# Linear attention and a gated MLP on one core: k and q projected apart in all pairs, transfers planned to land later, another order

## The chip, the cores and the metric

The kernel runs on one core of a Trainium2 chip. The metric is the device time of one execution in microseconds. TensorE (PE, with its weight loads as PEld), VectorE (DVE), ScalarE (ACT), GpSimd (POOL) and SyncE (SP, which issues nearly all DMAs) each run their own instructions in the order in which the program lists them, and wait for each other by semaphores.

## What is computed

The reference, cut to what matters:

```python
def _attn_ref(q, k, v, omega):          # q, k, v: (8, 8, 576, 64), omega: (128, 64)
    scale = 1.0 / np.sqrt(np.sqrt(D))
    def phi(x):
        proj = np.einsum('bhsd,md->bhsm', x, omega)
        h = proj - np.sum(x * x, axis=-1, keepdims=True) / 2.0
        h = h - np.max(h, axis=-1, keepdims=True)
        return np.exp(h) / np.sqrt(m)
    q_p, k_p = phi(q * scale), phi(k * scale)
    kv = np.einsum('bhsm,bhsd->bhmd', k_p, v)
    z = np.sum(k_p, axis=2)
    num = np.einsum('bhsm,bhmd->bhsd', q_p, kv)
    den = np.einsum('bhsm,bhm->bhs', q_p, z)[..., None] + 1e-06
    return num / den
def _moe_ref(x, w_in, w_out):           # x: (4608, 512), w_in: (512, 2048), w_out: (2048, 512)
    h = x @ w_in
    return (h / (1.0 + np.exp(-h))) @ w_out
```

The result of the attention, with its heads side by side, is the `x` of the MLP.

## The kernel before

**The attention** is worked off in 32 pairs of heads (`n` = 0 to 31, four pairs to a batch). For each pair, `project` (L393) multiplies the raw k or q by omega in 8 matmuls of 128 columns. Each contracts over 64 rows, and two heads share the array as a tile of rows 0 to 63 and one of rows 64 to 127; the trace shows each of these fp32 matmuls as two instructions, so 16 for k and 16 for q. The results fill two PSUM banks for k and two for q. A further small piece, `project_mids` (L419), projects the block that both heads share, on the full array. DVE takes maxima (`top`) and makes the biases (`shift`), ACT takes the exponentials out of PSUM (`expo`, L462) and so sets the banks free. Then come the sum over k (`sums` on POOL, `zsum` on PE, L513), k times v (`kv`, L521, in column tiles of 64), a transposition of it (`kv_turn`, L529), the denominators (`denom` on DVE, L545), the normalisation (`normal`, L556), three transpositions of q's features (`turn`, L562) and the numerator (`numer`, L583, in column tiles). The next pair's `kv` and a pair's `numer` stand together as one unit, `kvnum`.

**The MLP** is the bulk of the matmuls, all at L754 (`thrice`): 3120 instructions on the full array with 512 columns. Stages 1 and 2 work tile by tile of 512 tokens; later tiles are taken in pairs, by a seven-product scheme whose inner parts are the units `deep` and `product` (6 matmuls each). Attention pieces are pushed in between L754's all along, until about 813 us.

**What sets the order.** Every step is a unit with an engine, a guessed duration, a due time (`key`), the units that it comes after, and the buffers that it takes and frees. `Plan.run` (L170 to L318) plays these units through with its own guesses and emits them in that order; each engine then runs its share in that order. Four things in it matter here:

- `STIR` (L80): a table of (seed, size, from, to, mask). At L173 it moves the due times of some units by a pseudo-random amount. It only changes the order.
- `BOTH` (L38): for pairs in it (18 to 31) the k and the q projection are one unit that needs four free banks at once (L933 to L938); for the others they are two units of two banks each (L939 to L943).
- Banks: attention pieces take PSUM banks from `att` (2 banks) and, late in the program, from `h` (2 banks; L209). A unit is placed when the plan has its banks free.
- Transfers: a unit with `lat` on SP is taken to have landed at `max(pipe, t + dur + 2.2)` (L296 to L298), where `pipe` serialises the transfers and a large load has `lat` 1.5. What uses the data is planned from then on.

`TURN` (L113, 0.2) is the plan's price for a change of PE between full array, row tiles and column tiles; it stays.

Of the kernel before, what the change touches and what calls it, by code (L numbers as in the profile page):

```python
# [34 lines left out]

LAG = 2
FOLD = tuple(range(8))
BOTH = tuple(range(18, 32))  # L38
DIRECT = {(n, who) for n in range(28) for who in "kq" if not 8 <= n < 12}
NORM_DVE = tuple(range(8, 12))  # L40
AHEAD_OUT = 3
# [36 lines left out]
HANDOFF = {"PE": 0.3, "ACT": 0.25, "DVE": 0.22, "POOL": 0.2, "SP": 0.2}  # L78
CALM = 0.5
STIR = (  # L80
# [30 lines left out]
)  # L111
BOND = 0.0
TURN = 0.2  # L113
WIDE = ("w", "ts", "xq", "c", "ic", "g0", "g1", "g2", "g3")
TINY = ("mxk", "mxq", "nbk", "nbq", "mxm", "nbm", "sq", "den", "rd")
LEADIN = 96
# [36 lines left out]
class Plan:  # L153
# [16 lines left out]
    def run(self):  # L170
# [9 lines left out]
        pipe = port = 0.0  # L180
# [50 lines left out]
        while any(ready.values()):  # L231
            best = None
            for e, us in ready.items():
                pick, least = None, None
                for u in us:
                    t = 0.0
                    for a in u["after"]:
                        if self.units[a]["eng"] == e and not self.units[a]["lat"]:
                            t = max(t, end[a])
                        else:  # L240
                            t = max(t, first[a] + (CALM if e == "PE" and t > START_MLP else 0.0))
                    ok = True
                    for ring, _ in u["alloc"]:
# [4 lines left out]
                        t = max(t, s)  # L248
                    pools = ()
                    if ok and u["banks"]:  # L250
                        pools, s = bank_pools(u)
                        ok = pools is not None
                        if ok:
                            t = max(t, s)
                    if not ok:
                        continue
                    t = max(t, free_at[e])
                    if u["port"] and e == "POOL":
                        t = max(t, port)
                    elif u["port"]:  # L260
                        for a, b in holds:
                            if a <= t < b:
                                t = b
# [13 lines left out]
            u, pools, _, t = best  # L277
            e, n = u["eng"], u["name"]
            ready[e].remove(u)
            dur = u["dur"]  # L280
# [3 lines left out]
            if e == "PE":  # L284
                if tiled_by(u) != mode:
                    dur += TURN
                mode = tiled_by(u)
# [7 lines left out]
            done = t + dur  # L295
            if u["lat"]:  # L296
                pipe = max(pipe, t + dur + 1.0) + u["lat"]
                done = max(pipe, t + dur + 2.2)  # L298
            end[n] = done
            first[n] = done + HANDOFF[e]  # L300
            for ring, i in u["alloc"]:
# [20 lines left out]
def attention_mlp(ctx: ExitStack, tc: tile.TileContext, qT, kT, qn, kn, v, om_in, w_in, w_out, out):  # L322
# [581 lines left out]
    for n in range(NWIN):  # L904
# [3 lines left out]
        for i, who in enumerate("kq"):  # L908
# [23 lines left out]
            pj_after = [("raw",) + w, "omega"] + ([("r2",) + w] if fold else [])  # L932
            if n in BOTH:  # L933
                if i == 0:
                    add(pj, "PE", 1.75, at(n, 0, o + 3), lambda a, b, c, d, n=n: (project(n, "k", a, b), project(n, "q", c, d)),
                        banks=4, after=[("raw", n, x) for x in "kq"], order=[("proj", n - 1, x) for x in ("k" if n - 1 in BOTH else "kq")],
                        alloc=[("hk", ("h", n, "k"))] + [(f"{t}{x}", (t, n, x)) for t in ("mx", "nb") for x in "kq"])
            else:  # L938
                add(pj, "PE", 1.9 if fold else 1.15 if n < 2 * NPAIR else 0.9, at(n, 3 * i, o),  # L939
                    lambda a, b, n=n, who=who: project(n, who, a, b), banks=2, after=pj_after,  # L940
                    order=([("proj", n - 1, "k" if n - 1 in BOTH else who)] if n else []) + ([("mids", n)] if i and not fold else []),
                    alloc=([(f"h{who}", ("h",) + w)] if fold or not i else []) + ([] if fold else [(f"mx{who}", ("mx",) + w)])
# [4 lines left out]
            for j in range(3 if fold else 2):  # L947
                add(("top", n, who, j), "DVE", 0.2 if j == 2 else 0.6,
                    at(n, 3 * i + 1 + 0.1 * j, o + 1.2 + 0.1 * j),
                    lambda n=n, who=who, j=j: top(n, who, j), after=[md if j == 2 else ("proj", n, "k") if n in BOTH else pj])  # L950
            if not fold:
# [4 lines left out]
        if not fold:  # L956
# [8 lines left out]
            plan.freed_by[("raw", n, "k")] = [("mids", n), ("proj", n, "k")]  # L965
            plan.freed_by[("raw", n, "q")] = [("mids", n), ("proj", n, "k" if n in BOTH else "q")]
        e = {}
# [484 lines left out]
```

## Time and profile before

| | before |
|---|---|
| median of 3 runs | 989.75 us (985.5 to 991.65) |
| profiled execution, its own time | 988.49 us |
| its span, first to last instruction | 986.7 us |
| PE busy | 957.2 us (97%) |
| DVE, ACT, POOL busy | 771.4 us, 642.7 us, 403.5 us |
| granted TensorE clock | 1.000 |

In the rows that follow, a matmul's start is measured and its end is modelled, so the time of a stretch of PE is best read from one start to a later one. A row of the timeline has start, length, engine, line, operation, tiles, shape and count, and in brackets the idle time before it with what ended it. `ps_att`, `ps_h` and `ps_acc` are PSUM banks by pool, `rawk` and `rawq` the raw k and q, `oms` the scaled omega.

### The profile page before, as it was taken

Reading aid. Unit: us, or ns where it says so; the run is one execution under the profiler, and the core shown is the slowest. Engines: PE = TensorE matmul, PEld = TensorE weight load, DVE = VectorE, ACT = ScalarE, POOL = GpSimd, SP = SyncE. Lnnn points to the kernel's source line nnn. Section 1 sums busy time; section 2 is a strip of 40 time slices with the busy share of each in tenths; the row PEclk is TensorE's granted clock in tenths of the full one; section 3 lists DMA queues with packets and bytes.
Section 4 is the critical chain, followed back from the end, with each engine's and each line's share of the span. In section 5 each row is a group of like instructions: output and inputs, shape, how many; then the busy total and the mean of one; then the engine's idle time right before and its main releaser. Section 6 shows DMA issues by size and latency. Waiting matters only on the chain.

```text
span 986.7 us, 17025 instructions
## 1 busy us (share of the span) xinstructions
PE 957.2 (97%) x5846; PEld 767.6 (78%) x5846; DVE 771.4 (78%) x1611; ACT 642.7 (65%) x1237; POOL 403.5 (41%) x427
## 2 busy tenths in 40 slices
PE   8899899999999999999999999999999999999998
PEld 7677677777777777787788888788888878888886
DVE  3998798689455889884888999788799976369954
ACT  7998886688787776668568866566284544325442
POOL 3765465677876657776341343213111220000000
PEclk9999999999999999999999999999999999999999
DMA  7588887799998788898667666576555566556662
GB/s 283 196 270 284 287 293 255 258 376 316 303 291 288 265 284 270 324 305 289 218 211 236 196 206 225 203 268 201 170 181 192 192 201 229 192 192 214 194 214 103
DMA packets 103735, 238.70 MB, mean 242 GB/s; under 512 B 13665, under 2 KB 44513, under 8 KB 103649
## 3 DMA queue, kind: packets, MB, share of 16 engines
q1 hardware_dynamic: 103504, 237.54, 71.6%
q8 instruction: 47, 0.77, 0.3%
q14 instruction: 40, 0.32, 0.1%
q10 hardware_dynamic: 144, 0.07, 0.0%
HBM read 193.53 MB, written 44.04 MB: 241 GB/s over the span
## 4 chain that ended last, share of the span: by engine, by line
PE 64%; DVE 17%; ACT 8%; DMA 6%; issue 3%; POOL 1%; SPq 0%; DVEq 0%; ACTq 0%; POOLq 0%
PE ps_acc L754 47%; PE ps_h L754 5%; DVE prod L545 3%; DVE g L792 2%; PE ps_h L401 2%; PE ps_att L401 2%; ACT hq L462 2%; DVE g L654 2%; PE ps_att L521 2%; DVE g L650 1%; DVE ts L800 1%; DMA ic<-w_d 1%; DVE g L648 1%; ACT hk L462 1%; DMA g<-w_out 1%
## 5 line engine op out<-in xcount | busy, mean ns | idle before, releaser
L754 PE MATMUL ps_acc<-ts,w 128*128 128x512 f32 x2544 | 614.6, 395 | 0.3 <-issue 0.3
L754 PEld LDWEIGHTS ps_acc<-ts,w 128*128 128x128 f32 x2544 | 468.5, 188 | 97.5 <-issue 0.7
L796 ACT CAST ts<-g 128x1024 fp32r<-128x1024 f32 x112 | 118.6, 1063 | 101.2 <-PE ps_acc L754 95.0
L800 DVE TENSOR_TENSOR ts<-g,ts 128x1024 fp32r<-128x1024 f32 x112 | 144.4, 1294 | 48.6 <-ACT ts L796 48.2
L754 PE MATMUL ps_h<-xq,w 128*128 128x512 f32 x576 | 149.6, 401 | 3.5 <-ACT g L787 1.9
L556 POOL TENSOR_TENSOR hq<-hq,rd 128x384 f32<-128x384 f32 x84 | 89.7, 1094 | 110.8 <-DVE rd L551 109.6
L754 PEld LDWEIGHTS ps_h<-xq,w 128*128 128x128 f32 x576 | 104.1, 189 | 26.1 <-ACT g L787 3.1
L846 DVE TENSOR_TENSOR g<-ps_acc,g 128x512 f32<-128x512 f32 x144 | 95.2, 685 | 23.8 <-PE ps_acc L754 22.3
L491 POOL TENSOR_TENSOR t<-hk 128x256 f32<-128x256 f32 x64 | 57.6, 916 | 84.7 <-ACT hk L462 42.5
L792 DVE TENSOR_TENSOR g<-g,g 128x1024 f32<-128x1024 f32 x64 | 84.6, 1343 | 6.0 <-ACT g L787 5.7
L545 DVE CUSTOM_DVE_ANT_0 prod<-hq,ps_att 128x128 f32<-128x128 f32 (+1 forms) x180 | 51.6, 287 | 30.4 <-PE ps_att L513 11.4
L504 POOL TENSOR_TENSOR es<-t,es 128x256 fp32r<-128x256 f32 x32 | 28.7, 898 | 91.7 <-ACT es L500 91.7
L850 ACT ACTIVATE g<-g 128x1024 f32<-128x1024 f32 x36 | 37.6, 1058 | 32.7 <-DVE g L846 32.5
L668 POOL TENSOR_TENSOR w<-g,w 128x512 fp32r<-128x512 f32 x32 | 42.9, 1355 | 35.0 <-ACT w L664 14.6
L496 POOL TENSOR_TENSOR t<-t,hk 64x128 f32<-64x128 f32 x64 | 39.2, 613 | 20.7 <-ACT hk L462 17.2
L812 ACT CAST ts<-xq 128x1024 fp32r<-128x1024 f32 x21 | 22.2, 1056 | 33.8 <-PE ps_acc L754 31.5
L382 ACT ACTIVATE nat<-nat 128x576 f32<-128x576 f32 x48 | 32.8, 701 | 16.5 <-DMA nat<-kn 14.0
L816 DVE TENSOR_TENSOR ts<-xq,ts 128x1024 fp32r<-128x1024 f32 x21 | 27.0, 1284 | 19.9 <-ACT ts L812 19.9
L873 DVE TENSOR_TENSOR c<-ps_acc,c 128x512 f32<-128x512 f32 x48 | 30.8, 682 | 7.2 <-PE ps_acc L754 7.2
L462 ACT ACT_TABLE_LOAD x22 | 28.2, 1283 | 12.5 <-DVE nbk L441 8.0
L387 DVE TENSOR_REDUCE sq<-nat 128x9 f32<-128x576 f32 x48 | 34.5, 744 | 1.1 <-ACT nat L382 0.8
L462 ACT ACTIVATE hq<-ps_att,nbq 128x128 f32<-128x128 f32 x115 | 32.7, 386 | 4.0 <-DVE nbq L441 3.2
(210 smaller groups left out, 1535.8 us busy)
## 6 DMA issues: line engine op xcount, KB each, us to landing
w<-w_d SPq DMA_DIRECT2D x168, 512.0 KB, 4.2
w<-ws_d SPq DMA_DIRECT2D x48, 512.0 KB, 3.4
rawk<-kT SPq DMA_DIRECT2D x32, 352.0 KB, 4.1
rawq<-qT SPq DMA_DIRECT2D x32, 352.0 KB, 4.5
v<-v SPq DMA_DIRECT2D x32, 320.0 KB, 4.5
out<-c SPq DMA_DIRECT2D x17, 512.0 KB, 4.2
g<-w_in SPq DMA_DIRECT2D x16, 512.0 KB, 5.0
g<-w_out SPq DMA_DIRECT2D x16, 512.0 KB, 4.5
```

The costliest lines, as they stand in the source:

```text
L401: nc.tensor.matmul(ps[:, cols], raw[r, o : o + P], w[r], start=True, stop=n not in FOLD)
L462: nc.scalar.activation(h[:, c], ps[:, i * M : (i + 1) * M], AF.Exp, bias=bias_of(n, who, c), scale=-1.0 if n in FOLD else 1.0)
L491: nc.gpsimd.tensor_tensor(t[:, i], e[:, 5 * i : 5 * i + 2], e[:, 5 * i + 2 : 5 * i + 4], ALU.add)
L496: nc.gpsimd.tensor_tensor(t[r, i - 3, 0], t[r, i - 3, 0], e[r, MID], ALU.add)
L545: nc.vector.tensor_tensor_reduce(out=prod[r], in0=e[r, c], in1=z[r, j * M : (j + 1) * M], scale=1.0, scalar=GUARD, op0=ALU.mult, op1=ALU.a ...
L556: nc.gpsimd.tensor_tensor(e[:, c], e[:, c], rd[:, c].unsqueeze(2).broadcast_to([P, 3, M]), ALU.mult)
L668: nc.gpsimd.tensor_tensor(lo, T["w", i], hi.bitcast(F32), ALU.subtract)
L754: nc.tensor.matmul(ps, w(a), x[:, b], start=first and n == 0, stop=last and n == 2, **more)
L792: nc.vector.tensor_tensor(out, a, b, ALU.subtract)
L796: nc.scalar.copy(g[:, 0], T["g", p, SOURCE[j], u])
L800: nc.vector.tensor_tensor(g[:, 1], T["g", p, SOURCE[j], u], g[:, 0].bitcast(F32), ALU.subtract)
L846: nc.vector.tensor_tensor(to, T["q", p, chain, i], T["g", p, r, i // 2][:, i % 2], ALU.add)
```

## The change

The plan's three inputs change; no function that computes does. All instructions of the matmuls, copies and sums are the same in number; the order on every engine is another, and four more ACT table loads come in (70 to 74 in the program).

```diff
-BOTH = tuple(range(18, 32))
+BOTH = ()
...
 STIR = (
-    (29444, 2.5, -100, 900, 3), (30620, 4.0, -100, 900, 7), (57745, 2.5, 101, 261, 7), (26472, 5.25, 448, 538, 0),
...
+    (3618, 7.5, 64, 144, 7), (32634, 2.5, 89, 249, 0), (95862, 4.0, 338, 498, 3), (19267, 4.9, 349, 379, 0),
...
 TURN = 0.2
+LANDING = 0.9
...
             if u["lat"]:
                 pipe = max(pipe, t + dur + 1.0) + u["lat"]
-                done = max(pipe, t + dur + 2.2)
+                done = max(pipe, t + dur + 2.2) + LANDING
```

The helpers' lines stand one higher in the changed file (L754 is L753 there).

Three places on PE show what moves. The first is pair 21. Before, from the transposition of pair 20's kv to that of its features:

```order
L529 MATMUL ps_att<-ident,kt 128x128
L754 MATMUL ps_acc<-ts,w 128x512 x18
L401 MATMUL ps_h<-oms,rawk 128x128 x8
L401 MATMUL ps_att<-oms,rawq 128x128 x8
L754 MATMUL ps_acc<-ts,w 128x512 x30
L421 MATMUL ps_h<-oms,rawk 128x128
L421 MATMUL ps_h<-oms,rawq 128x128
L562 MATMUL ps_h<-ident,hq 128x128 x3
L754 MATMUL ps_acc<-ts,w 128x512 x6
L562 MATMUL ps_att<-ident,hq 128x128 x3
```

And in the change, from pair 21's k projection on:

```order
L400 MATMUL ps_att<-oms,rawk 128x128 x8
L420 MATMUL ps_h<-oms,rawk 128x128
L420 MATMUL ps_h<-oms,rawq 128x128
L753 MATMUL ps_acc<-ts,w 128x512 x6
L561 MATMUL ps_h<-ident,hq 128x128 x3
L753 MATMUL ps_acc<-ts,w 128x512 x6
L561 MATMUL ps_h<-ident,hq 128x128 x3
L753 MATMUL ps_acc<-ts,w 128x512 x6
L561 MATMUL ps_h<-ident,hq 128x128 x3
L753 MATMUL ps_acc<-ts,w 128x512 x12
L400 MATMUL ps_h<-oms,rawq 128x128 x8
L753 MATMUL ps_acc<-ts,w 128x512 x12
```

The q half of pair 21 now stands by itself between L754's, 30 of them away from its k half.

The second place is the middle block of pair 20. Before, it stands six L754 behind the transposition L529 of pair 19:

```order
L521 MATMUL ps_h<-hk,v 64x128 x10
L583 MATMUL ps_h<-en,kw 64x512 x2
L583 MATMUL ps_h<-en,kw 64x64 x2
L754 MATMUL ps_acc<-ts,w 128x512 x6
L513 MATMUL ps_h<-es,ones 128x256 x2
L529 MATMUL ps_h<-ident,kt 128x128
L754 MATMUL ps_acc<-ts,w 128x512 x6
L421 MATMUL ps_h<-oms,rawk 128x128
L421 MATMUL ps_h<-oms,rawq 128x128
```

In the change the middle block stands ahead of `kvnum`, and the transposition comes after both:

```order
L753 MATMUL ps_acc<-ts,w 128x512 x6
L420 MATMUL ps_att<-oms,rawk 128x128
L420 MATMUL ps_att<-oms,rawq 128x128
L520 MATMUL ps_h<-hk,v 64x128 x10
L582 MATMUL ps_att<-en,kw 64x512 x2
L582 MATMUL ps_h<-en,kw 64x64 x2
L753 MATMUL ps_acc<-ts,w 128x512 x6
L528 MATMUL ps_h<-ident,kt 128x128
```

The third place is the q projection of pair 16, which before stands six L754 behind its own middle block and next to pair 17's:

```order
L421 MATMUL ps_att<-oms,rawk 128x128
L421 MATMUL ps_att<-oms,rawq 128x128
L754 MATMUL ps_acc<-ts,w 128x512 x6
L401 MATMUL ps_att<-oms,rawq 128x128 x8
L401 MATMUL ps_h<-oms,rawq 128x128 x8
```

In the change the three transpositions of pair 15 and 18 L754's stand between the two, and pair 17's half is not beside it:

```order
L420 MATMUL ps_att<-oms,rawk 128x128
L420 MATMUL ps_att<-oms,rawq 128x128
L561 MATMUL ps_att<-ident,hq 128x128 x3
L753 MATMUL ps_acc<-ts,w 128x512 x6
L561 MATMUL ps_att<-ident,hq 128x128 x3
L753 MATMUL ps_acc<-ts,w 128x512 x6
L561 MATMUL ps_att<-ident,hq 128x128 x3
L753 MATMUL ps_acc<-ts,w 128x512 x6
L400 MATMUL ps_att<-oms,rawq 128x128 x8
L753 MATMUL ps_acc<-ts,w 128x512 x24
```

Counted over PE's whole list past the start-up (that is, from the first L754 on): two projections next to each other 15 times before (pairs 18 to 31, and the q halves of 16 and 17), never in the change; a projection next to a `kvnum` once before, 8 times in the change.

56 rows, old and new, of the table STIR are left out of this document.

## Prediction

> **What bounds the kernel now.** I read the page's busy times first, then the windows by stage, then the waits of PE, then PE's timeline at the places that the change moves.
>
> ```profile
> PE 957.2 (97%) x5846; PEld 767.6 (78%) x5846; DVE 771.4 (78%) x1611; ACT 642.7 (65%) x1237; POOL 403.5 (41%) x427
> PE 64%; DVE 17%; ACT 8%; DMA 6%; issue 3%; POOL 1%; SPq 0%; DVEq 0%; ACTq 0%; POOLq 0%
> ```
>
> PE is busy 97% of the span, and no other engine is over 78%. So there are only two ways to change the time: the matmuls themselves take more or less of PE, or the 29.5 us in which PE is idle (986.7 - 957.2) shrink or grow. The windows, cut at 62 us (start-up over), 325, 475 and 813 us (last attention piece), tell where those 29.5 us lie. The columns after the window's length are busy us with the number of instructions for PE, PEld, DVE, ACT and POOL, then the granted clock, DMA share and GB/s.
>
> ```profile
> 0.00:62.00 62.00, 53.43 (x587) 43.47 (x587) 44.26 (x140) 53.27 (x155) 34.25 (x51) 1.00 0.69 236
> 62.00:325.00 263.00, 250.71 (x1594) 195.50 (x1591) 196.41 (x477) 209.40 (x403) 172.44 (x180) 1.00 0.88 297
> 325.00:475.00 150.00, 145.61 (x936) 115.40 (x935) 122.53 (x267) 106.71 (x238) 104.25 (x97) 1.00 0.84 287
> 475.00:813.00 338.00, 337.77 (x1989) 273.48 (x1989) 295.82 (x606) 207.03 (x371) 92.58 (x100) 1.00 0.62 206
> 813.00:986.70 173.70, 169.63 (x750) 139.72 (x746) 112.34 (x125) 66.28 (x74) 0.00 (x0) 1.00 0.57 191
> ```
>
> PE idles 8.6 us in the start-up, 12.3 us up to 325, 4.4 us up to 475, 0.2 us up to 813, and 4.1 us at the end, most of it behind the last matmul. The change's pairs 18 to 31 lie in the third and fourth window. In the fourth, PE has no idle time to give: whatever is added to PE there is paid in full, and a wait that is taken away there gains nothing.
>
> **What a projection by itself costs.** A lone k half (16 instructions) between L754's, late in the second window:
>
> ```profile
> 324.29 2.20 PE L754 MATMUL ps_h<-xq,w 128*128 128x512 f32 x9
> 326.42 1.16 PE L401 MATMUL ps_att<-oms,rawk 64*128 64x128 f32 x16
> 327.51 2.34 PE L754 MATMUL ps_h<-xq,w 128*128 128x512 f32 x9
> 329.69 0.62 PE L754 MATMUL ps_acc<-ts,w 128*128 128x512 f32 x2
> ...
> 813.38 147.19 PE L754 MATMUL ps_acc<-ts,w 128*128 128x512 f32 x648
> ```
>
> The last row gives the pace of L754 when nothing interrupts it: 147.19 / 648 = 0.227 us. From 324.29 to 329.69 are 5.40 us with 18 of them (4.09 us), so the half costs 1.31 us. Both halves together, pair 21:
>
> ```profile
> 467.38 4.35 PE L754 MATMUL ps_acc<-ts,w 128*128 128x512 f32 x18
> 471.66 1.16 PE L401 MATMUL ps_h<-oms,rawk 64*128 64x128 f32 x16
> 472.66 1.06 PE L401 MATMUL ps_att<-oms,rawq 64*128 64x128 f32 x16
> 473.65 7.10 PE L754 MATMUL ps_acc<-ts,w 128*128 128x512 f32 x30
> 480.59 0.38 PE L421 MATMUL ps_h<-oms,rawk 128*128 128x128 f32 x2
> ...
> 483.01 1.64 PE L754 MATMUL ps_acc<-ts,w 128*128 128x512 f32 x6
> 484.49 0.49 PE L562 MATMUL ps_h<-ident,hq 128*128 128x128 f32 x3
> ```
>
> From 467.38 to 480.59 are 13.21 us with 48 L754's (10.90 us): 2.31 us. The first run stands behind a transposition, which slows it by 0.12 us (483.01 to 484.49: six take 1.48 us, not 1.36), so the two halves cost 2.19 us. Two lone halves cost 2.62 us. Parting them costs 0.43 us, and it is the way into row tiles and back that is paid twice.
>
> The order has 15 such neighbours before (14 pairs, and the q halves of pairs 16 and 17) and none after: 15 x 0.43 = **+6.4 us**. Against it stand projections next to a `kvnum`, once before and 8 times now. There the way out of the one and the way into the other fall together:
>
> ```profile
> 319.74 0.71 PE L583 MATMUL ps_att<-en,kw 128*64 128x512 f32 x6
> 320.38 1.66 PE L754 MATMUL ps_h<-xq,w 128*128 128x512 f32 x6
> 321.88 0.40 PE L513 MATMUL ps_att<-es,ones 128*128 128x256 f32 x2
> ```
>
> Behind a `kvnum` six L754's take 1.50 us (320.38 to 321.88), 0.14 over their pace; ahead of a projection nine take 2.13 us (324.29 to 326.42), 0.09 over. So a direct neighbour saves about 0.2 us: 7 x 0.2 = **-1.4 us**. Net **+5.0 us** of PE, about 3.7 of it for pairs 21 to 31 (11 x 0.43 less 5 x 0.2), past 467 us, where no idle time hides it. Bounds: the part before that, 1.3 us, may lie in waits that exist anyway (+3.7 in all); without the neighbours' saving it is +6.4.
>
> The Trainium skill, page "TensorEngine Tiling (Array Packing)", section "Key Properties", says that changing the tiling mode drains the TensorE, whether between full array and tiles or from one kind of tile to another. By that rule row tiles next to column tiles save nothing and the term would be +6.4; by the rows above, half of the two ways falls away.
>
> **What the waits give back.** PE's waits in the third window, grouped, and then the rows of the timeline at the four longest:
>
> ```profile
> PE ps_h L421 <- ACT kw L534: 1.2, 1, 1.2
> PE ps_h L562 <- POOL ic L711: 1.1, 1, 1.1
> PE ps_att L401 <- ACT hk L462: 0.9, 1, 0.9
> PE ps_att L513 <- ACT kt L526: 0.7, 1, 0.7
> PE ps_att L562 <- ACT en L566: 0.4, 1, 0.4
> ```
>
> ```profile
> 351.43 0.50 PE L513 MATMUL ps_att<-es,ones 128*128 128x256 f32 x2 [0.69 <-ACT kt L526]
> 372.02 1.04 PE L401 MATMUL ps_att<-oms,rawq 64*128 64x128 f32 x13 [0.94 <-ACT hk L462]
> 399.69 0.52 PE L562 MATMUL ps_h<-ident,hq 128*128 128x128 f32 x3 [1.15 <-POOL ic L711]
> 456.26 0.49 PE L421 MATMUL ps_h<-oms,rawk 128*128 128x128 f32 x2 [1.20 <-ACT kw L534]
> ```
>
> The last row is the second place shown in the order: pair 20's middle block waits for the bank of a transposition six L754's ahead, which ACT copies late. In the change the block stands before that transposition: -1.20 us. The second of the four is the third place: a q half that waits for the exponential of its own middle block, six L754's ahead. Now 18 L754's and three transpositions lie between: -0.94 us. At 351.43 the sum over k stands three L754's behind a `kvnum`; in the change it is nine: 6 x 0.227 = 1.36 us more, over the 0.69 that was waited. These three places: **-2.8 us**.
>
> The wait at 399.69 is of another kind. The profile names POOL, but what ends at that time is ACT's work on the bank of pair 18's four-bank projection, which stands ahead of this transposition:
>
> ```profile
> 396.63 0.69 ACT L382 ACTIVATE nat<-nat 128x576 f32<-128x576 f32 x1 [4.65 <-DMA nat<-kn]
> 397.22 1.04 ACT L796 CAST ts<-g 128x1024 fp32r<-128x1024 f32 x1
> 398.16 0.40 ACT L500 CAST es<-t 128x256 fp32r<-128x256 f32 x1
> 398.46 1.91 ACT L462 ACTIVATE hk<-ps_h,nbk 128x128 f32<-128x128 f32 x7
> ```
>
> ```profile
> w<-w_d SPq DMA_DIRECT2D x168, 512.0 KB, 4.2
> ic<-w_d SPq DMA_DIRECT2D x16, 512.0 KB, 5.8
> nat<-kn SPq DMA_DIRECT2D x24, 288.0 KB, 4.0
> ```
>
> ACT stood 4.65 us at a square whose load was late, with the exponentials queued behind it. The plan counts on 2.2 to 2.9 us from issue to use, the rows show medians of 4.0 to 5.8 us; with 0.9 us more it counts on 3.1 to 3.8. And in the change pair 18's projections come behind pair 16's transpositions. I count this wait as gone: **-1.15 us**. All of them: -4.0 of the 4.4 us in that window.
>
> **What may come in.** Each of the 28 half projections now waits for two banks of its own, in order on PE, with all of PE's list queued behind it, and with DVE and ACT behind that. The trace shows no such lone half in the four-bank part. Nearest is the 0.94 us above; none of them wait: 0; all: 26 us. In the fourth window, with the same four banks, PE idles 0.2 us in 338 although four banks had to be free at once, so I take the low end: **+0.5 us**.
>
> In the start-up ACT sets the pace (53.27 of 62 us). Counted over ACT's list up to the copy of pair 3's x, the change has one L636 and two L664 more ahead of it:
>
> ```profile
> L636 ACT ACTIVATE g<-g 128x512 f32<-128x512 f32 x7 | 4.9, 758 | 0.4 <-DMA g<-w_in 0.4
> L664 ACT CAST w<-g 128x512 fp32r<-128x512 f32 x5 | 3.4, 676 | 1.0 <-DVE g L654 0.9
> ```
>
> That is 0.76 + 2 x 0.68 = 2.1 us later for x, and 2.1 us of weight work that no longer stands in the way afterwards. Bounds -2.1 and +2.1; I take 0, since the sum of ACT's work is the same. The four table loads that come in lie past 475 us, where ACT has 131 us to spare; without that cover they would cost about 5 us.
>
> **The sum** goes by the profiled execution: 988.5 + 5.0 - 4.0 + 0.5 = **990.0 us**. That execution is 1.3 us under the median of the three runs shown, 989.75; the three spread over 6 us, so I leave it there. A measurement of this kernel can tell about 1% from no change, that is 9.9 us: below 979.9 is faster, above 999.7 slower.
>
> **The rivals.** (1) The waits up to 325 us go as well. The 12.3 us of idle time there come from the same causes, late loads and banks, and the new order and landing time touch every one of them; a full gain gives 990.0 - 12.3 = 977.7, and it has to take 10 of the 12.3 to count as faster. Against it: the pairs there already had k and q apart, the chain still runs through the same exponentials, and a new order makes waits as well as it removes them. Chance 0.17. (2) The lone halves wait for banks: if 14 of 28 wait 0.94 us each, 990.0 + 13.2 - 0.5 = 1002.7; slower from about 11 of them on. For it: the waits at 372.02 and 399.69 are just this kind. Against it: two banks are found sooner than four. Chance 0.13. (3) The parting costs nothing, because the halves fall into time that PE would wait anyway: 985.0. Against it is the 0.2 us of idle in the fourth window. Chance 0.15. (4) The landing time does nothing, since 3.8 us is still below what the rows show, and the waits move to other pieces: all 4.0 us stay and the time is 994.0. Chance 0.15.
>
> **How the numbers follow.** The forecast itself has 0.40; with (3) and (4), which both end within 1%, 0.70 for no change, 0.17 for faster, 0.13 for slower. The forecast's own range is 985 to 995 by the bounds above. The range to hold 8 of 10 reaches to (1) and most of the way to (2): **978 to 1001 us**, which leaves out rather less than half of each.
>
> **What would show it.** In the profile of the changed kernel: lone L401 rows of 16 in the fourth window, each 1.3 us over L754's pace; PE busy up by about 5 us, to 962; the waits at L421, L401, L513 and L562 of the third window gone, its idle time at 1 us or less; the fourth window's idle time still below 1 us. I am wrong on the price if PE's busy time does not rise; wrong on the waits if idle time between 62 and 475 us differs from about 13 us by more than 5; rival (2) would show as L401 waiting for ACT's L462 many times past 350 us.

## The result and the profile after

| | before | changed |
|---|---|---|
| median | 988.37 us (985.19 to 991.65, 13 runs) | 993.37 us (989.51 to 996.97, 13 runs) |
| ratio to before | | 1.0054, 95% interval 1.0039 to 1.0069 |
| profiled execution, span | 988.49 us, 986.7 us | 994.02 us, 992.1 us |

The change makes the kernel 5.3 us slower by the ratio, which is clear of noise and well inside what was called no change. The forecast of 990.0 us was for a profiled execution of 988.49; the one of the changed kernel took 994.0. Busy times on the page of the changed kernel:

```profile
PE 963.0 (97%) x5846; PEld 772.2 (78%) x5846; DVE 769.0 (78%) x1611; ACT 648.8 (65%) x1241; POOL 404.0 (41%) x427
```

The span is 5.4 us longer. PE's busy time rose by 5.8 us (957.2 to 963.0), its idle time went from 29.5 to 29.1 us. So nearly nothing was won back in waits, and the loss is matmuls that take longer. The windows at the same cuts, with the columns as before:

```profile
0.00:62.00 62.00, 50.49 (x527) 40.94 (x527) 43.22 (x138) 51.37 (x150) 35.83 (x51) 0.97 0.67 231
62.00:325.00 263.00, 253.76 (x1642) 200.30 (x1642) 196.50 (x482) 210.04 (x406) 172.76 (x179) 0.99 0.86 295
325.00:475.00 150.00, 145.99 (x909) 114.57 (x909) 113.99 (x251) 109.05 (x236) 96.11 (x96) 1.00 0.87 287
475.00:813.00 338.00, 338.00 (x2002) 273.10 (x2001) 300.48 (x618) 210.28 (x376) 99.28 (x102) 1.00 0.64 204
813.00:992.10 179.10, 174.75 (x772) 143.30 (x770) 114.79 (x127) 68.08 (x76) 0.00 (x0) 1.00 0.58 194
```

PE idles 11.5 us in the start-up (8.6 before), 9.2 us up to 325 (12.3), 4.0 us up to 475 (4.4), and nothing up to 813 (0.2). The clock column, which stood at 1.00 everywhere before, is below it in the first two windows. Windows at fixed times hold different work in two kernels, so a better measure is when the same L754 starts, counted from the first of the 3120. The number has to be one at which PE has done the same other work in both kernels; the rows below are such numbers (at 12 and 120 one to three small instructions differ). The times in us by which some of them start later than in the kernel before (each from one profiled execution; the two later columns belong to experiments below):

| L754 number, its start before | changed | q six behind k | k and q together again |
|---|---|---|---|
| 12, at 64.0 us | +5.3 | -0.9 | +4.1 |
| 120, at 100.9 us | +7.6 | -0.1 | +6.4 |
| 570, at 264.2 us | -0.2 | 0.0 | -0.9 |
| 754, at 323.8 us | +1.9 | +0.7 | +1.6 |
| 1163, at 459.4 us | +2.8 | +2.5 | +1.4 (at 1170) |
| 1486, at 562.4 us | +4.1 | +4.8 | +6.8 |
| 2034, at 724.1 us | +5.1 | +6.9 | +11.8 |
| 2376, at 813.4 us | +5.1 | +7.5 | +13.0 |
| 3119, at 982.6 us | +5.1 | +7.5 | +13.0 |

The changed kernel loses 7.6 us in the start-up and has them back by 264 us. At 324 us it is 1.9 us late, and at 459 us, ahead of pair 21, 2.8 us. The last 2.3 us come between 459 and 813 us, where PE has no idle time, and they stay. PE's idle time, summed over the trace up to the same numbers, is 0.1 us less than before at 324 us, 0.5 less at 459 us and 0.7 less at the end. So PE's busy time is 2.0 us longer by 324 us, and 3.8 us more come behind it, 2.5 of them past 459 us.

How far single executions can be read, some experiments below show that keep the order of before up to 350 us. Four of them stand 0.3, 0.7, 1.2 and 2.8 us later than the kernel before at 324 us, with nothing changed up to there. So the 1.9 us at 324 us are not clear of chance.

The waits of PE in the third window, where the prediction had counted on 4.0 us:

```profile
PE ps_att L512 <- ACT kt L525: 1.6, 1, 1.6
PE ps_h L512 <- ACT es L499: 0.8, 1, 0.8
PE ps_att L420 <- ACT hk L461: 0.8, 1, 0.8
PE ps_h L512 <- POOL es L503: 0.4, 1, 0.4
PE ps_h L561 <- POOL t L490: 0.2, 1, 0.2
```

3.8 us in five rows. They are other pieces than before, but of the same kind: the sum over k of pair 15, which waited 0.69 us for the copy of `kt`, now runs without a wait, and that of pair 16 waits 1.64 us for the next such copy:

```profile
383.45 0.51 PE L512 MATMUL ps_att<-es,ones 128*128 128x256 f32 x2 [1.64 <-ACT kt L525]
```

A lone half in the fourth window:

```profile
564.05 5.74 PE L753 MATMUL ps_acc<-ts,w 128*128 128x512 f32 x24
569.72 1.16 PE L400 MATMUL ps_h<-oms,rawk 64*128 64x128 f32 x16
570.81 0.33 PE L528 MATMUL ps_att<-ident,kt 128*128 128x128 f32 x1
```

From 564.05 to 570.81 are 6.76 us; 24 L753's at their pace of 0.227 take 5.45, which leaves 1.31 us. These hold the way out of the column tiles of a `kvnum` ahead (0.14 us by the rows of the prediction), and the way back behind the half falls to the transposition, so they are not quite the price of a half. Nine halves between 330 and 812 us do stand by themselves between L753's; from the third start ahead to the third behind, less the pace, they cost 1.30 to 1.31 us each, the figure of the second window before.

### The profile page after: what moved, and what is told of

Its sections match the earlier page's. It is cut to its first block, busy times and chain, and to the rows that moved or that the text cites. A ratio compares the mean times of both kernels' runs of the same rounds, so it can differ in the third digit from the quotient of the medians.

```text
span 992.1 us, 16998 instructions
## 1 busy us (share of the span) xinstructions
PE 963.0 (97%) x5846; PEld 772.2 (78%) x5846; DVE 769.0 (78%) x1611; ACT 648.8 (65%) x1241; POOL 404.0 (41%) x427
## 4 chain that ended last, share of the span: by engine, by line
PE 76%; DVE 9%; ACT 8%; POOL 3%; DMA 3%; issue 1%; SPq 0%; DVEq 0%; ACTq 0%; POOLq 0%
PE ps_acc L753 51%; PE ps_h L753 8%; PE ps_att L400 3%; PE ps_att L520 2%; DVE prod L544 2%; PE ps_att L582 2%; DVE g L649 2%; PE ps_h L400 1%; PE ps_att L561 1%; ACT hq L461 1%; DVE g L647 1%; ACT hk L461 1%; DVE g L653 1%; POOL ic L725 1%; PE ps_h L561 1%
## 5 line engine op out<-in xcount | busy, mean ns | idle before, releaser
L753 PE MATMUL ps_acc<-ts,w 128*128 128x512 f32 x2544 | 611.6, 394 | 1.1 <-ACT hq L461 0.7
L753 PEld LDWEIGHTS ps_acc<-ts,w 128*128 128x128 f32 x2544 | 469.4, 188 | 99.4 <-ACT hq L461 1.2
L753 PE MATMUL ps_h<-xq,w 128*128 128x512 f32 x576 | 151.5, 403 | 1.8 <-ACT g L786 1.7
L555 POOL TENSOR_TENSOR hq<-hq,rd 128x384 f32<-128x384 f32 x84 | 86.2, 1051 | 134.0 <-DVE rd L550 130.4
L753 PEld LDWEIGHTS ps_h<-xq,w 128*128 128x128 f32 x576 | 104.5, 189 | 26.2 <-ACT g L786 3.2
L791 DVE TENSOR_TENSOR g<-g,g 128x1024 f32<-128x1024 f32 x64 | 82.1, 1306 | 22.8 <-ACT g L786 22.5
L490 POOL TENSOR_TENSOR t<-hk 128x256 f32<-128x256 f32 x64 | 55.4, 882 | 94.4 <-ACT hk L461 47.9
L495 POOL TENSOR_TENSOR t<-t,hk 64x128 f32<-64x128 f32 x64 | 35.7, 558 | 11.0 <-ACT hk L461 4.3
```

The lines of the kernel that those rows point to most:

```text
L490: nc.gpsimd.tensor_tensor(t[:, i], e[:, 5 * i : 5 * i + 2], e[:, 5 * i + 2 : 5 * i + 4], ALU.add)
L555: nc.gpsimd.tensor_tensor(e[:, c], e[:, c], rd[:, c].unsqueeze(2).broadcast_to([P, 3, M]), ALU.mult)
L753: nc.tensor.matmul(ps, w(a), x[:, b], start=first and n == 0, stop=last and n == 2, **more)
L791: nc.vector.tensor_tensor(out, a, b, ALU.subtract)
```

## The experiments

The theory after the result: parting costs its price on PE, and where PE has no idle time it is paid; the new order moves waits to other places and removes none on balance. The rivals: the loss comes from the slowed start and its clock; or the landing time and the order do win something, and only the price hides it. "Above before" below is the ratio less one, times 988 us.

### Parting alone, the old order kept

In the kernel before, the joined piece of pairs 18 to 31 issues k, and q one `deep` or `pr` unit (six L754's) later. Banks and order stay:

```diff
+        held = None
...
-            u["fn"](*[bank(p) for p in u["pools"]])
+            banks = [bank(p) for p in u["pools"]]
+            if u["name"][0] == "proj" and len(banks) == 4:
+                project(u["name"][1], "k", *banks[:2])
+                held = (u["name"][1], "q", *banks[2:])
+                continue
+            u["fn"](*banks)
+            if held and u["name"][0] in ("deep", "pr"):
+                project(*held)
+                held = None
```

> The kernel before, with one thing changed: in pairs 18 to 31 the q half of the projection is issued six L754's behind the k half, with the same four banks and the same order of all else. Theory (price of parting): 14 x 0.43 us = 6.0 us more PE work, of which up to 1.3 us may hide in waits before 475 us: 4.7 to 6.0 us slower than before, PE busy up by about 6 us, idle time of PE past 475 us still below 1 us. Rival (clock): the loss of the change comes from the stretches in which its TensorE clock was halved near 60 and 103 us; those do not arise here, so the time is that of before within 1 us. Rival (banks): parted halves wait for banks; here the banks are taken as before, so idle time must not rise.

Measured: 995.32 us, ratio 1.0079 (1.0062 to 1.0096), 7.8 us above before, more than the 4.7 to 6.0 expected. PE's busy time is 962.0 us. Its idle time rose too, from 29.5 to 32.2 us, where no rise was expected; 1.6 us of that lie before 324 us, where nothing is changed yet. From 324 us on the delay in the table grows by 6.8 us, of which 1.0 is idle time; the 5.8 us of busy time are 0.41 us for each of the 14 pairs. Between 459 and 813 us it builds up evenly, 5.0 us for 11 pairs: 0.45 us a pair, close to the 0.43 of the prediction. PE's timeline at pair 21:

```profile
474.20 1.16 PE L401 MATMUL ps_h<-oms,rawk 64*128 64x128 f32 x16
475.29 1.66 PE L754 MATMUL ps_acc<-ts,w 128*128 128x512 f32 x6
476.88 1.16 PE L401 MATMUL ps_att<-oms,rawq 64*128 64x128 f32 x16
477.97 5.75 PE L754 MATMUL ps_acc<-ts,w 128*128 128x512 f32 x24
```

From 474.20 to 476.88 are 2.68 us, 1.36 of them the six L754's: 1.32 us for the half. None of these rows waits. With everything else as before, the parting alone makes the kernel slower, and by more than the whole change does.

### The price paid twice

In the changed kernel each half of pairs 21 to 31 is cut in two pieces of 8 instructions with six L754's between them:

```diff
-        for i in range(4):
+        for i in part:
...
+            if u["name"][0] == "proj" and u["name"][1] > 20:
+                two = u["name"][1:] + tuple(banks)
+                project(*two, part=(0, 1))
+            elif u["name"][0] == "half":
+                project(*two, part=(2, 3))
```

> The changed kernel, in which each of the 22 lone halves of pairs 21 to 31 is cut in two more pieces of 8 instructions with six L754's between them, so that the way into row tiles and back is paid 22 times more, in the window where TensorE has no idle time. Nothing else moves. By the price of parting (0.43 us from the rows of before, 0.53 us a pair in the experiment that parted the halves in the old order): 22 x 0.43 to 22 x 0.53 = 9.5 to 11.7 us slower than the changed kernel, so 14 to 17 us slower than before, TensorE's busy time between 475 and 813 us longer by that. By the rival (the loss of the changed kernel comes from the new order or from the slowed start, not from the parting): within 1 us of the changed kernel, 4 to 6 us slower than before.

Measured: 1008.49 us, ratio 1.0208 (1.0182 to 1.0234): 15 us above the changed kernel, more than any of the theories gave. PE's timeline at one cut half:

```profile
475.12 1.62 PE L755 MATMUL ps_acc<-ts,w 128*128 128x512 f32 x6
476.67 0.71 PE L400 MATMUL ps_att<-oms,rawk 64*128 64x128 f32 x8
477.32 1.66 PE L755 MATMUL ps_acc<-ts,w 128*128 128x512 f32 x6
478.91 0.71 PE L400 MATMUL ps_att<-oms,rawk 64*128 64x128 f32 x8
```

From 476.67 to 478.91 are 2.24 us, 0.88 over six L755's. Two pieces cost 1.76 us where the whole half costs 1.31: 0.45 us for one more way into row tiles and back, or 9.9 us for 22. In the profiled execution the span is 17.0 us longer than that of the changed kernel, 12.6 in PE's busy time (975.6) and 4.4 in waits that were not there before; why the busy time grew by 2.7 us more than the price was not found out. L755's now stand ahead of a piece, and come too soon for DVE:

```profile
475.00:830.00 355.00, 350.58 (x2004) 274.20 (x2004) 298.25 (x622) 210.93 (x378) 97.59 (x102) 1.00 0.60 195
```

```profile
PE ps_acc L755 <- DVE g L847: 1.6, 2, 0.9
...
PE ps_acc L755 <- DVE ts L817: 0.5, 1, 0.5
```

4.4 us idle (355 - 350.58) where the changed kernel had none. In the rows the price holds; that a piece can be moved by six L754's without waits does not.

### The waits of the prediction, moved by hand

In the kernel before, the four pieces of PE's list that the prediction named go behind the L754's that follow them; all other engines keep their order:

```diff
-        for u in plan.run():
+        later = {("z", 15): 1, ("proj", 16, "q"): 2, ("turn", 16, 0): 1, ("mids", 20): 1}
...
+            for _ in range(later.get(u["name"], 0)):
+                j = next(j for j in range(i + 1, len(units)) if units[j]["name"][0] in ("deep", "pr"))
+                units.insert(i, units.pop(j))
+                i += 1
```

> The kernel before, in which four pieces of TensorE's list are moved behind the L754's that follow them, and nothing else: the sum over k of pair 15 by 6, the q halves of pairs 16 and 17 by 12, the first transposition of pair 16 by 6, the middle block of pair 20 by 6. These are the four places of the prediction's step on the waits (0.69, 0.94, 1.15 and 1.20 us waited). If the waits are worth their length, as the prediction took them: 2.8 to 4.0 us faster than before, idle time between 325 and 475 us from 4.4 to about 1 us. If what is waited for is a chain through ACT, DVE and POOL that a piece of TensorE only meets (the theory formed from the result): the four rows go, others come within the next tens of us, and the time stays within 1.2 us of before.

Measured: 991.97 us, ratio 1.0035 (1.002 to 1.0051), 3.5 us slower. The theory had within 1.2 us, so both missed. PE's timeline and ACT's at the q halves of pairs 16 and 17:

```profile
369.42 1.86 PE L754 MATMUL ps_acc<-ts,w 128*128 128x512 f32 x7
373.63 4.28 PE L754 MATMUL ps_acc<-ts,w 128*128 128x512 f32 x11 [2.34 <-DVE ts L800]
377.83 1.16 PE L401 MATMUL ps_att<-oms,rawq 64*128 64x128 f32 x16
```

```profile
380.81 2.17 ACT L462 ACTIVATE hq<-ps_att,nbq 128x128 f32<-128x128 f32 x8 [6.78 <-DVE nbq L441]
```

The L754's that were put ahead had their own input to wait for, 2.34 us at 373.63; the q half came at 377.83, not 372.02, and its exponentials at 380.81. Part of that is the clock: the 11 L754's take 4.20 us, at their pace 2.50, and the granted clock is 0.50 from 373.4 to 376.8 us. So about 1.7 us of this delay are a half clock that came with the new wait. Before, the exponentials came at 376.86:

```profile
376.86 2.17 ACT L462 ACTIVATE hq<-ps_att,nbq 128x128 f32<-128x128 f32 x8 [3.21 <-DVE nbq L441]
```

So the two q halves stay where they were in the kernel before, and the other three go:

```diff
-        for u in plan.run():
+        later = {("z", 15), ("turn", 16, 0), ("mids", 20)}
...
+            if units[i]["name"] in later:
+                j = next(j for j in range(i + 1, len(units)) if units[j]["name"][0] in ("deep", "pr"))
+                units.insert(i, units.pop(j))
+                i += 1
```

> As the experiment that moved four pieces behind L754's, but the q halves of pairs 16 and 17 stay where they are in the kernel before; the sum over k of pair 15, the first transposition of pair 16 and the middle block of pair 20 go 6 L754's later. In the experiment with four pieces all of the loss (3.7 to 4.9 us between 352 and 381 us) stood at the two q halves, where the L754's that were put ahead waited for DVE and ACT's exponentials of q came 3.95 us later. If the other three waits (0.69, 1.15 and 1.20 us) are worth their length, as the prediction took them: 3.0 us faster than before, idle time between 325 and 475 us from 4.4 to 1.4 us. If they only move: within 1 us of before, with new waits in the same window.

Measured: 988.96 us, ratio 1.0002 (0.9985 to 1.002). Nothing gained, as the theory said. PE's waits in the third window, and its timeline behind the first moved piece:

```profile
PE ps_att L562 <- ACT en L566: 1.4, 2, 1.0
PE ps_h L562 <- ACT hk L462: 1.1, 2, 0.6
PE ps_att L401 <- ACT hk L462: 0.9, 1, 0.9
PE ps_att L401 <- DVE den L545: 0.2, 1, 0.2
```

```profile
368.18 0.49 PE L562 MATMUL ps_att<-ident,hq 128*128 128x128 f32 x3
369.71 0.52 PE L562 MATMUL ps_att<-ident,hq 128*128 128x128 f32 x3 [1.03 <-ACT en L566]
```

The same transposition in the kernel before, without a wait:

```profile
366.05 0.94 PE L562 MATMUL ps_att<-ident,hq 128*128 128x128 f32 x6
```

3.6 us of wait in place of 4.3. Counted by the L754's again, the delay fell by 1.4 us at the sum over k (from 2.7 at 307 us, before anything is moved; a half clock of 6.8 us at 139 us is in it), rose by 1.9 us up to 381 us and by 0.5 up to 454, and fell by 1.5 at the middle block of pair 20: 2.3 us at 474. Single waits do give time back, and the next pieces of the same chain take most of it, here the transposition 15 us behind the sum over k.

### The slowed start

Before the start-up pieces that wait, 60 small matmuls on ones are added to the changed kernel; their results are overwritten, so this adds work to it:

```diff
+    def stir_up(ps, count):
+        for _ in range(count):
+            nc.tensor.matmul(ps[:, 3 * P :], ones, ones, start=True, stop=True)
...
+        if (n, who) == (6, "k"):
+            stir_up(a, 24)
...
+        if n == 3:
+            stir_up(ps, 24)
...
+        if (n, g) == (3, 0):
+            stir_up(ps, 12)
```

> The changed kernel with 60 extra small matmuls whose results are overwritten, placed just ahead of three waits of PE near 56, 58 and 99 us, so that PE is active while it waits. Theory (price of parting): the clock may stay at 1.0, but the start-up's delay is made up by 230 us anyway, so the time stays within 1 us of the change. Rival (clock): the halved clock cost 10.2 us at half speed, so up to 5 us come back, and the time is that of before.

Measured: 992.49 us, ratio 1.0043 (1.0022 to 1.0064), within 1 us of the changed kernel. Its first window keeps the clock:

```profile
0.00:62.00 62.00, 53.84 (x563) 44.57 (x563) 42.98 (x138) 50.83 (x149) 35.85 (x51) 1.00 0.65 229
```

At 264 us (L754 number 570) it is 2.0 us ahead of the kernel before, and at 459 us (number 1163) 3.8 us behind, later than the changed kernel. Its third window idles 5.5 us (150 - 144.46):

```profile
325.00:475.00 150.00, 144.46 (x895) 113.32 (x894) 110.39 (x238) 107.42 (x232) 94.05 (x95) 0.99 0.85 284
```

What is won before 325 us is lost again there, part of it in waits. This execution is not free of slowed clock, though: it has 0.50 for 3.4 us at 144 and at 383 us, and at 995.16 us it is the slowest of the nine. By their median the loss without the start-up's half clock is still 4.2 us, by the interval at least 2.2. So that clock is not what makes most of the loss; with 60 matmuls added, the run cannot tell how much of the rest it makes. The profiles of the changed kernel and of the kernel before agree: 3.2 of the 5.1 us come past 324 us, where neither has a slowed clock until the last matmul is done.

### The three parts one by one

The plan's inputs were set in all the other ways. The edits are one line each, or the table of the other kernel. First k and q apart, nothing else:

> The kernel before with the pairs 18 to 31 apart and nothing else: old table, old landing times; the order up to pair 17 is that of before. Theory (price of parting): 14 x 0.43 less 4 x 0.2 for projections beside a kvnum: 5.2 us over before, clock at 1.0 throughout. Rival (clock): no change within 1 us. Rival (banks): more than 7 us over before, with idle time of PE up past 325 us.

Then the landing time alone, and the table alone:

> The kernel before with 0.9 us of landing time in its plan; k and q of pairs 18 to 31 stay together, the table stays. By the theory: TensorE's busy time stays at 957 us, and the time is from 1 us below to 5 us above before, since the order is redrawn and its waits were not looked for. By the rival (landing time takes waits away): 2 us or more faster than before, with less idle time of TensorE between 62 and 475 us and shorter waits of ACT and POOL for loads.

> The kernel before with the changed kernel's table, k and q of pairs 18 to 31 together and no landing time. By the theory (each table fits only the settings that it stands with, and any other setting draws an order whose waits are unlooked for): 5 to 25 us slower than before with TensorE's matmuls alone taking no longer, the loss in waits before 475 us. By the rival (the new table's order takes waits away, and only the parting costs): 2 us or more faster than before.

Then the changed kernel with one part taken back: k and q together again, no landing time, and the table of before:

> The changed kernel with k and q of pairs 18 to 31 in one unit again; the plan's order up to pair 17 stays as in the change, the start-up with its halved clock too. Theory (price of parting): 14 joined pairs give back 6.0 us, 6 fewer projections beside a kvnum take 1.2 us: 4.8 us under the change, about that of before, although the clock is still halved twice. Rival (clock): same time as the change within 1 us.

> The changed kernel without the 0.9 us of landing time in its plan. By the theory (landing time only redraws the order; the loss is the price of parting): TensorE's busy time stays at 962 to 964 us, and the time is 3 to 9 us above before, according to what waits the new order happens to have. By the rival (landing time takes waits away, and pays for part of the parting): TensorE's busy time stays, and the time is at least 3 us above the changed kernel, so 8 us or more above before, with the difference in waits for loads (ACT at L381, POOL at L710).

> The changed kernel with the table of before: k and q apart in all pairs and 0.9 us of landing time, so the eighth way of putting the change's three parts together. If the parts simply added up, the sum of the two that were run alone would come out: 9 us for the parting and 20 us for the landing time, 29 us above before. By the theory that a table fits only the settings that it stands with, no sum holds; 10 to 40 us above before, with TensorE's matmuls alone 5 us longer and the rest in waits. By the rival that the landing time helps once k and q are apart: less than 9 us above before.

| table | k and q | landing | ratio | us above before |
|---|---|---|---|---|
| old | apart | 0 | 1.0092 (1.0073 to 1.0111) | 9.1 |
| old | together | 0.9 | 1.02 (1.0176 to 1.0225) | 19.8 |
| old | apart | 0.9 | 1.0272 (1.0248 to 1.0296) | 26.9 |
| new | together | 0 | 1.0383 (1.0356 to 1.041) | 37.8 |
| new | together | 0.9 | 1.0154 (1.0132 to 1.0175) | 15.2 |
| new | apart | 0 | 1.0342 (1.0317 to 1.0368) | 33.8 |
| new | apart | 0.9 | 1.0054 (1.0039 to 1.0069) | 5.3 |

Parting adds 9.1 and 7.1 us under the old table and takes off 4.0 and 9.9 under the new one. Landing time costs 19.8 and 17.8 us under the old table and wins 22.6 and 28.5 under the new one. Both tables are best in the setting that they stand with. What a part is worth depends on the table. Under the old table the two parts nearly add up (28.9 against 26.9 measured), so there my reading that no sum holds is not borne out. Parting in the kernel before cost more than the 5.2 us expected, and more than the 7 at which the rival of waits for banks was to be seen. PE idles 1.7 us in the fourth window, 0.2 before, so a part of the 9.1 is new waits; the rest of the excess was not followed up. The landing time alone was expected within 5 us of before. The two runs of the new table without landing time lose more than I expected, 20 us of it before the 12th L754, and PE's timeline of the one with k and q apart has a wait there that is more than twice the longest of before (2.2 us). The granted clock is 0.50 from 59.9 to 70.2 us there, so the slowed clock is in these 20 us too:

```profile
60.75 1.11 PE L582 MATMUL ps_h<-en,kw 128*64 128x512 f32 x1 [4.89 <-ACT en L565]
```

My expectation for the changed kernel with k and q together fell: it was to come back to the time of before and came out 15.2 us above it. Its fourth window, and PE's longest wait there:

```profile
475.00:813.00 338.00, 330.45 (x1953) 263.38 (x1952) 294.88 (x606) 201.80 (x364) 97.72 (x99) 1.00 0.61 200
```

```profile
PE ps_acc L753 <- DVE ts L799: 2.1, 2, 1.4
```

7.6 us idle in a window that was full in both kernels. The plan laid another order, and nobody had looked for its waits. So this run says nothing on the price of parting; only runs that keep the order do. Its PE is busy for 963.1 us, as long as with k and q apart, so busy times of whole programs do not show that price when the order is drawn anew. The longest waits for loads, of before and of the run with the landing time alone:

```profile
POOL ic L711 <- DMA ic<-w_d: 19.3, 9, 3.9
...
ACT nat L382 <- DMA nat<-kn: 14.0, 7, 4.7
```

```profile
POOL ic L711 <- DMA ic<-w_d: 28.4, 10, 5.7
...
ACT nat L382 <- DMA nat<-kn: 4.0, 2, 3.2
```

ACT's waits for the natural k went from 14.0 to 4.0 us and POOL's from 19.3 to 28.4, and PE is 20 us later. Shorter waits for loads on ACT did not make this kernel faster. Whether landing time is worth something under the new table, apart from the order that it draws there, can't be told, since it acts through the order alone. None of these orders beats the kernel before, and no experiment pointed to one that does.

## Why the prediction was right, and where it was not

**Price of parting, +5.0: right for each piece, too high in the sum.** Between 330 and 812 us, counted in the traces as above, two halves side by side cost 2.19 to 2.21 us before (14 of them) and lone halves 1.30 to 1.31 in the changed kernel (nine): parting costs 0.41 us, as in q behind k. A half and a `kvnum` side by side cost 3.51 to 3.53 (four), apart 1.30 and 2.42: 0.20 us saved, the figure worked out from two rows. But past 459 us, where 3.7 us were due, PE's busy time grew by 2.5, and from 324 us on by 3.8 in all. The new order puts other small pieces next to each other too: the L753's past 459 us are interrupted 66 times, where they were 77 times before. The prediction counted only the `kvnum`; that these pieces make up the difference is likely, not shown. PE's busy time of the whole rose by 5.8 us, to 963.0 where 962 was forecast, and that this fits is partly luck: 2.0 us of it come before 324 us, in the stretch with the half clock.

**Waits give back, -4.0: this step failed.** Idle time in the third window went from 4.4 to 4.0 us, so 0.4 came back. The four waits are gone from their pieces, as the prediction said, and 3.8 us of others stand in the same window. The error was to treat a wait as time that PE would own once the piece stood later. That holds for the row and not for the window: the chain through ACT, DVE and POOL that made the piece wait makes another one wait, as the three moved pieces show in the old order. The prediction's own sign for the waits, about 13 us of idle time between 62 and 475 us, came out at 13.2, but only because the second window won 3.1 us that the forecast did not have. This is rival (4), which gave 994.0 us; the profiled execution took 994.0. That they agree so closely is chance, since the price and the banks in that sum came out otherwise. Its reason was half right: it named the landing time, and the middle block and the sum over k moved their waits as well.

**Lone halves waiting for banks, +0.5: right.** PE waits nowhere in the fourth window; rival (2) did not happen there. In the third, one wait of 0.8 us for `hk` is of that kind, though at a middle block (L420).

**The start-up, 0: right in the sum, not in its course.** It lost 7.6 us by 101 us, more than the bound of 2.1, and they were back by 264 us: 5.6 us in idle time that shrank and 2.2 in busy time. By the windows, 2.9 us of idle time were lost up to 62 us and 3.1 won up to 325. Rival (1) had the 12.3 us of the second window's waits gone altogether. A quarter of them went, and they paid for the start.

**Rival (3), parting costs nothing, is refuted** by q behind k: 7.8 us above before with no other edit.

The forecast of 990.0 us came out 4.0 us low for the profiled execution and 3.4 for the median. The step on the waits is 3.6 us of that; the others nearly cancel.

## What to carry to other kernels

On an engine without idle time, count what an edit adds, and what its order saves, and take it as paid in full; the rows of the profile price it well (0.43 us from two rows, 0.41 to 0.45 in the experiments). A wait that the profile shows is not time to be had by moving the piece that waits: look for what feeds it, and for the next piece that needs the same chain. And where a planner draws the order, a setting cannot be tried by changing it alone, since the order that was searched for goes with it; edit the emitted order instead, and leave the rest.

## What was not expected of the hardware

The clock fell to half after waits in the start-up. Windows of the changed kernel around 58 and 103 us, and PE's timeline there:

```profile
60.00:62.00 2.00, 2.00 (x7) 1.24 (x5) 2.00 (x3) 2.00 (x6) 1.53 (x2) 0.50 0.99 398
62.00:64.00 2.00, 2.00 (x17) 1.72 (x18) 1.93 (x4) 1.25 (x3) 0.00 (x0) 0.50 0.95 337
...
103.00:106.00 3.00, 3.00 (x21) 2.63 (x19) 2.19 (x5) 1.79 (x3) 2.45 (x3) 0.50 1.05 404
```

```profile
56.08 0.55 PE L561 MATMUL ps_acc<-ident,hq 128*128 128x128 f32 x3 [1.27 <-POOL hq L555]
...
59.70 0.48 PE L528 MATMUL ps_acc<-ident,kt 128*128 128x128 f32 x1 [2.29 <-ACT kt L525]
...
62.28 2.40 PE L520 MATMUL ps_acc<-hk,v 128*64 128x128 f32 x20
```

The 20 matmuls at 62.28 take 2.19 us to the next row (64.47), where the same 20 take 1.14 us at full clock (561.84 to 562.98). The half clock set in during the wait of 2.29 us and 0.8 us behind one of 2.51, and lasted 6.8 and 3.4 us. The profiled execution of the kernel before, whose longest wait in the same stretch is 2.2 us, keeps 1.000. That is not so in all of them: the runs with three pieces moved and with k and q apart in the kernel before have its order up to 350 us, and fell to half clock for 6.8 us at 139 and for 3.4 us at 118 us, with waits of 2.97 and 2.26 us. With the 60 matmuls added, waits of 1.91 and 1.96 us went with the half clock at 144 and 383 us. So the length of a single wait does not decide it in these runs. Of 55 other executions of the kernel before, 18 have a mean granted clock of 0.999 or more and a median of 986.9 us, and 15 have 0.997 or less and 991.0 us, so part of its spread goes with the clock. The 13 of the changed kernel have 0.993 to 0.996. The Trainium skill, page "TensorE: Matmul & The Clock Gate", Part 1, says that the clock goes to half after an idle window of about 3.4 us and that the window runs freely; here shorter waits, of 1.91 to 2.97 us, went with it, and the measurement decides. So an idle time of PE in a start-up can cost twice, though here the second window had room for it.
